# Seven half-width products in seven blocks instead of three, k's exponential in SBUF, and a written-out order, in a linear-attention plus feed-forward kernel

## The chip, the cores and the metric

The kernel runs on one core of one Trainium2 chip. The metric is the device time of one execution in microseconds; the figure used is the median of the runs. Engines are named as in the profile: PE (TensorE matmul), PEld (TensorE weight load), DVE (VectorE), ACT (ScalarE), POOL (GpSimd) and SP (SyncE, which issues the DMAs).

## The reference

Two stages. The first is a recurrence over 768 time steps for 4 batches and 8 heads of 48 dimensions, with a decay `w` between 0.8 and 0.95; the second a feed-forward layer from 384 to 2048 and back with a leaky ReLU.

```python
state = zeros((B, H, D, D))                      # B, H, S, D = 4, 8, 768, 48
for t in range(S):
    cur = einsum('bhd,bhe->bhde', u * k[:, :, t], v[:, :, t])
    y[:, :, t] = einsum('bhd,bhde->bhe', r[:, :, t], state + cur)
    state = w[:, :, t, :, None] * state + einsum('bhd,bhe->bhde', k[:, :, t], v[:, :, t])
x = y.transpose(0, 2, 1, 3).reshape(3072, 384)
h = x @ w_in                                      # 384 -> 2048
out = maximum(0.01 * h, h) @ w_out                # 2048 -> 384
```

## The kernel before, in words

**Chunks.** The 3072 rows are 24 chunks of 128 time steps. The first four chunks are done as two pairs (`pair`), the other twenty alone (`single`). In a single chunk, ScalarE takes the logarithm of w (L855), PE sums it over time (`cum`, L861, and totals, L864) into a PSUM bank `cp`, VectorE adds the logarithm again into `ci` in SBUF (L873), and ScalarE makes three exponentials: of the totals (`a`, L882), of `cp` in place (L887), and of `-ci` into a second PSUM bank, `ek` (L891). VectorE multiplies r by `cp` and k by `ek` into the two halves of `rk` (both in the helper `mult`, L545). `rk` is transposed into `rkT`, either on PE (L556) with a copy, or, for the 13 chunks in `RK_DMA`, by a DMA transpose that SP issues (L908). PE makes the scores (L1002; for chunks in `MERGED` two chunks at once), VectorE masks them (two masks per chunk, L932), and PE makes the state's sums (L942) and the output from state and masked scores (L968, L973). GpSimd works beside this: the bonus of u from products with k and r in a tile `ru` (L575, L579), reduced by VectorE into `dg` (L583) and multiplied by v into `vs` (L587), the cast of v (`vb`, L595), and the decayed state `sb` (L919). VectorE adds `vs` to the output (L618); the result is transposed into `xT`, on PE (L604) or by DMA (L987, chunks in `Y_DMA`).

**Feed-forward blocks.** The chunks are put into 15 blocks of one or two chunks (`blocks`). For each, 16 slices of the hidden layer are made by PE (`up`, L1168, 128 columns for a single, 256 for a pair), ScalarE applies the leaky ReLU into `g` (L1183), and PE makes the output of each chunk by 16 matmuls of 384 columns (`down`, L1198), copied out by VectorE or ScalarE (L1209, L1211) and stored (L1215).

**Seven products.** The last three pair blocks (`SEVEN_LAST = 3`) take `seven` instead of `down`. The pair's output is a product of a 2 x 2 arrangement of blocks (two chunks, two halves of the hidden slices) with another (two halves of the hidden slices, two halves of the 384 columns). It is made from seven products of halves instead of eight, each of 8 matmuls of 192 columns (L1098), at the price of four sums of 1024 columns on VectorE for each block (L1079), of three copies (L1112, L1114) and five adds (L1119) of 192 columns, and, once in the kernel, of four differences of the halves of w_out (`mix`, L1048). The sums and differences lie in tiles of the pool `in`, which otherwise holds loads.

**Weights and lead.** w_in is loaded in six pieces and w_out in four, between the loads of the pairs, and cast by VectorE, ScalarE or GpSimd (L488 to L492). Until the first blocks can run, PE is given matmuls of zeros where the plan sees a hole (L1240).

**The order.** Every operation is a step of a class `Plan`, with a cost per engine, a priority, its inputs and the buffers that it reads and takes. `Plan.order` runs a list scheduler over these costs: at each free engine it takes the ready step of the best priority, changed by a table of 1090 offsets (`RANK`), and a table `FORCE` fixes the engine of some steps. The result is the program order of each engine; each engine runs its own list in order, and SP's list is the order of the DMAs. A step that waits therefore holds everything behind it on its engine.

Of the kernel before, what the change touches and what calls it, by code (L numbers as in the profile page):

```python
# [8 lines left out]
F32 = mybir.dt.float32  # L9
BF16 = mybir.dt.bfloat16  # L10
# [5 lines left out]
class Buf:  # L16


    def __init__(self, pool, kind=None, wide=1):
        self.wide = wide  # L20
        self.pool, self.kind, self.users, self.t, self.free_at = pool, kind or pool, [], None, 0.0


class Plan:


    ENGINES = ("PE", "DVE", "ACT", "POOL", "SP")
# [4 lines left out]
    def __init__(self, limits, slack_from, slack, late):  # L32
        self.steps, self.limits, self.late = [], limits, late
        self.slack_from, self.slack = slack_from, slack
# [8 lines left out]
    def order(self, pools):  # L43
        n = len(self.steps)
        users = [[] for _ in range(n)]
        left = [len(s[3]) for s in self.steps]
        for i, s in enumerate(self.steps):
            for j in s[3]:
                users[j].append(i)
        bufs = {}  # L50
        for i, s in enumerate(self.steps):
            for b in (*s[4], *s[5]):
                bufs[id(b)] = b
        remain = {k: len(b.users) for k, b in bufs.items()}
        free_tiles = {p: [(0.0, k) for k in range(len(t))] for p, t in pools.items()}
        in_use = {}
        ready_at = [0.0] * n
        self.start, self.done, self.eng = [None] * n, [0.0] * n, [None] * n
        free = dict(self.BEGIN)
        ready = {e: [] for e in self.ENGINES}  # L60
        events = []
        dma_free, flying = 0.0, []

        def offer(i, t):
            for e in self.steps[i][0]:
                heapq.heappush(events, (t, 0, e, i))

        for i in range(n):
            if not left[i]:
                offer(i, 0.0)  # L70
        for e in self.ENGINES:
            heapq.heappush(events, (free[e], 1, e, -1))
        count, out = 0, []
        while events:
            now, kind, e, i = heapq.heappop(events)
            same = {e}
            if kind == 0 and self.start[i] is None:
                heapq.heappush(ready[e], (self.steps[i][2], i))
            elif kind == 2:
                in_use[i] -= 1  # L80
# [231 lines left out]
def kernel(  # L312
# [13 lines left out]
    L = 128  # L326
# [948 lines left out]
```

## Time and profile before

| | |
|---|---|
| time, median of 3 runs | 179.23 us (179.16 to 179.73) |
| span of the profiled execution | 177.7 us |
| the profiled execution's own time | not listed by itself; the median lies 1.5 us above the span |
| PE busy | 170.7 us, 96% |
| PE weight loads busy | 133.9 us, 75% |
| VectorE busy | 133.9 us, 75% |
| ScalarE busy | 115.6 us, 65% |
| GpSimd busy | 105.3 us, 59% |
| granted TensorE clock | full throughout |
| DMA | 34.24 MB, mean 193 GB/s |

Matmuls are pipelined and their modelled ends overlap the next one's start, so a busy PE is not PE at its peak. In a line of the timeline the first number is the start, the second the time until the end of the last merged instruction, and brackets hold the idle time before it and what ended that. In a group, the number after the comma is the mean duration of one instruction in ns. A line of the chain that ended last has a start, a length and what ran. "DMA to landing" is the time from issue to arrival.

### The profile page before, as it was taken

The page shows a single profiled execution, that of the slowest core. Times are in us where ns is not written, and L with a number is a line of the kernel's source. Part 1 is how long each engine was busy: PE and PEld are TensorE (multiplying, and loading weights), DVE is VectorE, ACT ScalarE, POOL GpSimd, SP SyncE. Part 2 cuts the span into 40 slices and gives each one's busy share as a digit, 9 for nine tenths or more (in the row PEclk, how much of TensorE's full clock was granted, in tenths as well). Part 3 has the DMA queues.
Part 4 walks back from the last instruction along what each step waited for, and adds up shares of the span by engine and source line. Part 5 has one row for each costly group of instructions (what it writes and reads, how often), then busy time and mean ns, then how long its engine had stood idle before and what let it go on. Part 6 is the DMA issues. An engine that isn't in the chain of part 4 may idle for free.

```text
span 177.7 us, 5379 instructions
## 1 busy us (share of the span) xinstructions
PE 170.7 (96%) x2106; PEld 133.9 (75%) x2110; DVE 133.9 (75%) x268; ACT 115.6 (65%) x258; POOL 105.3 (59%) x139
## 2 busy tenths in 40 slices
PE   7899899999999999999999999999999999999993
PEld 2456678766879767797788776788777798899992
DVE  7599744568987949979968888699779688776463
ACT  5679877764856687487497891288873677662820
POOL 5998554255897749993905994659884099100000
PEclk9999999999999999999999999999999999999999
DMA  5999999999999999997999999997999996613004
GB/s 142 262 283 341 338 377 325 234 197 168 193 146 210 171 189 191 194 227 171 221 185 209 197 147 222 205 177 155 191 208 148 241 207 160 159 24 111 4 22 157
DMA packets 115884, 34.24 MB, mean 193 GB/s; under 512 B 108305, under 2 KB 115090, under 8 KB 115858
## 3 DMA queue, kind: packets, MB, share of 16 engines
q1 hardware_dynamic: 115856, 33.89, 94.3%
q8 instruction: 16, 0.26, 0.7%
q14 instruction: 10, 0.08, 0.2%
q10 hardware_dynamic: 2, 0.00, 0.0%
HBM read 25.17 MB, written 4.72 MB: 168 GB/s over the span
## 4 chain that ended last, share of the span: by engine, by line
PE 74%; DMA 8%; SPq 5%; ACT 4%; DVE 3%; issue 3%; POOL 1%; DVEq 0%; ACTq 0%; POOLq 0%
PE ps L1168 29%; PE ps L1198 23%; PE ps L1098 8%; DMA in<-in_moe_w_in_dram 5%; SPq L630 4%; DMA in<-in_w_dram 3%; PE ps L1002 3%; PE ps L973 2%; ACT g L1183 2%; PE ps L861 2%; PE ps L556 2%; PE ps L968 2%; PE ps L942 1%; PE ps L604 1%; DVE in L1048 1%
## 5 line engine op out<-in xcount | busy, mean ns | idle before, releaser
L1168 PE MATMUL ps<-xT,w_in_b 128*128 128x256 bf16 (+1 forms) x720 | 73.3, 251 | 0.1
L1183 ACT ACTIVATE g<-ps 128x512 bf16<-128x512 f32 x96 | 55.9, 594 | 22.4 <-PE ps L1168 19.5
L1168 PEld LDWEIGHTS <-w_in_b 128*128 128x128 bf16 x720 | 57.6, 98 | 8.4 <-issue 0.3
L1198 PE MATMUL ps<-w_out_b,g 128*128 128x384 bf16 x288 | 56.5, 326 | 0.0
L1198 PEld LDWEIGHTS <-g 128*128 128x128 bf16 x288 | 25.1, 97 | 12.0
L545 DVE TENSOR_TENSOR rk<-in,ps 128x384 bf16<-128x384 f32 x48 | 25.3, 550 | 8.0 <-ACT ps L887 3.0
L575 POOL TENSOR_TENSOR ru<-in,ub 128x384 f32<-128x384 f32 x24 | 25.4, 1061 | 6.2 <-DMA in<-in_k_dram 6.1
L932 DVE TENSOR_TENSOR m<-ps,maskb 128x512 bf16<-128x512 f32 x40 | 25.3, 682 | 4.2 <-PE ps L1002 3.3
L595 POOL CAST vb<-in 128x384 bf16<-128x384 f32 x24 | 13.2, 553 | 22.3 <-DMA in<-in_v_dram 19.1
L579 POOL TENSOR_TENSOR ru<-ru,in 128x384 f32<-128x384 f32 x24 | 24.4, 1028 | 2.9 <-DMA in<-in_r_dram 2.4
L587 POOL TENSOR_TENSOR vs<-in,dg 128x384 f32<-128x384 f32 x20 | 17.0, 852 | 3.5 <-DVE dg L583 2.9
L919 POOL TENSOR_TENSOR sb<-s,a 128x384 bf16<-128x384 f32 x18 | 14.9, 830 | 3.3 <-ACT a L882 3.3
L873 DVE TENSOR_TENSOR ci<-ps,lw 128x384 f32<-128x384 f32 x20 | 11.1, 553 | 4.5 <-PE ps L861 1.8
L618 DVE TENSOR_TENSOR y<-ps,vs 128x384 bf16<-128x384 f32 x20 | 10.9, 553 | 4.5 <-PE ps L973 4.5
L583 DVE TENSOR_REDUCE dg<-ru 128x8 f32<-128x384 f32 x24 | 13.1, 544 | 0.7 <-POOL ru L579 0.6
L882 ACT ACTIVATE a<-ps 64x4 f32<-64x4 f32 x36 | 6.1, 168 | 11.6 <-DVE ci L873 8.9
L855 ACT ACTIVATE lw<-in 128x384 bf16<-128x384 f32 x20 | 10.1, 520 | 3.8 <-DMA in<-in_w_dram 3.6
L891 ACT ACTIVATE ps<-ci 128x384 f32<-128x384 f32 x20 | 9.7, 485 | 1.8 <-DVE ci L873 1.8
L887 ACT ACTIVATE ps<-ps 128x384 f32<-128x384 f32 x20 | 9.3, 467 | 0.5 <-DVE ci L873 0.3
L1240 PE MATMUL ps<-zeros 128*128 128x128 bf16 (+1 forms) x31 | 7.6, 351 | 1.6 <-DVE zeros L409 1.3
L556 PE MATMUL ps<-ident,rk 128*128 128x128 bf16 x88 | 8.4, 220 | 0.5 <-DVE rk L545 0.4
L1098 PEld LDWEIGHTS <-g 128*128 128x128 bf16 x96 | 8.1, 98 | 0.2
(105 smaller groups left out, 222.5 us busy)
## 6 DMA issues: line engine op xcount, KB each, us to landing
out_dram<-o SPq DMA_DIRECT2D x23, 192.0 KB, 2.7
in<-in_w_dram SPq DMA_DIRECT2D x20, 192.0 KB, 4.6
in<-in_v_dram SPq DMA_DIRECT2D x20, 192.0 KB, 4.9
in<-in_r_dram SPq DMA_DIRECT2D x20, 192.0 KB, 4.4
in<-in_k_dram SPq DMA_DIRECT2D x20, 192.0 KB, 4.6
in<-in_moe_w_out_dram SPq DMA_DIRECT2D x4, 768.0 KB, 8.7
in<-in_moe_w_in_dram SPq DMA_DIRECT2D x4, 384.0 KB, 7.8
in<-in_moe_w_in_dram SPq DMA_DIRECT2D x2, 768.0 KB, 8.5
```

The source lines that it names most:

```text
L545: (nc.gpsimd if e == "POOL" else nc.vector).tensor_tensor(out=o, in0=x, in1=i, op=ALU.mult)
L575: lambda e: nc.gpsimd.tensor_tensor(out=ru.t[:], in0=kv(), in1=ubv, op=ALU.mult),
L579: lambda e: nc.gpsimd.tensor_tensor(out=ru.t[:], in0=ru.t[:], in1=rv(), op=ALU.mult),
L583: lambda e: nc.vector.tensor_reduce(out=dg.t[:], in_=ru.t[:], axis=AX.X, op=ALU.add),
L587: lambda e: nc.gpsimd.tensor_tensor(out=vs.t[:], in0=vv(), in1=dg.t[:].unsqueeze(2).to_broadcast([128, H, D]), op=ALU.mult),
L595: {"POOL": 0.56}, lambda e: nc.gpsimd.tensor_copy(out=vb.t[:], in_=vv()),
L919: lambda e: nc.gpsimd.tensor_tensor(out=sb.t[:].rearrange("p g a d -> p (g a) d"), in0=s_in.t[:].rearrange("p g a d -> p (g a) d"), in1=a_ ...
L932: lambda e, par=par: nc.vector.tensor_tensor(out=m.t[:, par, :, :], in0=sc[par].t[:].rearrange("p (g t) -> p g t", g=NP), in1=maskb[:].uns ...
L1098: nc.tensor.matmul(o(), lhsT=x()[:, i, :], rhs=y()[:, i, :], start=fresh, stop=(stop and i == ii[-1]), skip_group_check=True)
L1168: nc.tensor.matmul(hp.t[:, a * N : (a + 1) * N], lhsT=w_in_b[:, t, (j + a) * 128 : (j + a + 1) * 128], rhs=xT[:, t, c0 : c0 + N], start=(a ...
L1183: lambda e, hp=hp, g=g, j=j, J=J, N=N: nc.scalar.activation(out=g.t[:, j : j + J, 0:N], in_=hp.t[:, 0 : J * N].rearrange("p (a n) -> p a n ...
L1198: nc.tensor.matmul(op.t[:, 0:DM], lhsT=g.t[:, j, off : off + 128], rhs=w_out_b[:, j, :], start=(j == 0), stop=(j == NJ - 1))
```

## The change

- `SEVEN_LAST` goes from 3 to 7, and the two neighbouring single blocks become a pair, so the last seven of 14 blocks, all pairs, take `seven`.
- k's exponential is written back into `ci` in SBUF, and the bank `ek` is no longer taken. The product with k can then run on VectorE or on GpSimd. In the order that is written out, 12 of the 20 run on GpSimd.
- `Plan.order` no longer schedules. It walks a list `ORDER` of all 1124 steps and assigns buffers; `FORCE` is a new table. Its costs only set the matmuls of zeros and which buffer is taken.
- Buffers: `in` 10 to 11, `ci` 2 to 3, `g` 3 to 4; the pairs' transposed tiles are taken from `g`; `xT` is six tiles of one block each instead of one tile for all rows.

What follows in the program: PE has 480 up matmuls of 256 columns and 192 of 128 (before: 432 and 288), 160 down matmuls (288) and 392 half-width products (168). The four differences of w_out stand much earlier in VectorE's list. SP's list has the loads in another order: the second pair's w and r go ahead of v, and one of the two wide w_in pieces comes first of the weights, ahead of the narrow ones.

```diff
-        self.pool, self.kind, self.users, self.t, self.free_at = pool, kind or pool, [], None, 0.0
+        self.pool, self.kind, self.users, self.t, self.free_at, self.seen = pool, kind or pool, [], None, 0.0, {}
...
     def order(self, pools):
...
+        for i in ORDER:
+            engs, fn, deps, reads, takes, wire = self.steps[i][0], *self.steps[i][1:2], *self.steps[i][3:]
...
+            e = FORCE.get(i) or next(iter(engs))
+            now = max(at[e], ready[i])
...
-RANK = {0: -309.63, 1: -310.62, 2: -303.35, 3: -175.12, 4: -176.12, 5: -3.85, 6: -313.07, 7: -303.34, 8:
...
+ORDER = [0, 1, 4, 2, 3, 1122, 5, 6, 7, 11, 14, 20, 13, 21, 12, 18, 19, 8, 25, 22, 26, 27, 23, 24, 40, 36, 15,
...
-    SEVEN_LAST = 3
+    SEVEN_LAST = 7
...
-    blocks = [2, 1, 1, 1, 1, 2, 2, 2, 2, 2, 1, 1, 2, 2, 2]
+    blocks = [2, 1, 1, 1, 1, 2, 2, 2, 2, 2, 2, 2, 2, 2]
...
-    xT = pool.tile([128, KT, NCH * L], BF16, name="xT")
-
-    make("in", 10, [128, 1536], F32)
+
+    make("in", 11, [128, 1536], F32)
...
-    make("ci", 2, [128, H, D], F32)
+    make("ci", 3, [128, H, D], F32)
...
-    make("rkT2", 2, [128, 2 * NP, 256], BF16)
...
-    make("g", 3, [128, NJ, max(blocks) * L], BF16)
+    make("g", 4, [128, NJ, max(blocks) * L], BF16)
+    make("xT", 6, [128, KT, max(blocks) * L], BF16)
...
-            rkT = Buf("rkT2")
+            rkT = Buf("g", "rkT2")
...
-            ci, ek = Buf("ci"), Buf("ps", "ek")
+            ci = Buf("ci")
...
             s_ek = step(
                 {"ACT": 0.53},
-                lambda e: nc.scalar.activation(out=heads(ek.t), in_=ci.t[:], func=AF.Exp, scale=-1.0),
-                P0, deps=[s_ci], reads=[ci], takes=[ek])
+                lambda e: nc.scalar.activation(out=ci.t[:], in_=ci.t[:], func=AF.Exp, scale=-1.0),
+                P0, deps=[s_ci], reads=[ci])
...
             s_k = step(
-                {"DVE": 0.55}, lambda e: mult(rk.t[:, 1, :, 0:D], heads(ek.t), kv()),
-                P0, deps=[kl, s_ek], reads=[slot, ek], takes=[rk])
+                {"DVE": 0.55, "POOL": 1.0}, lambda e: mult(rk.t[:, 1, :, 0:D], ci.t[:], kv(), e),
+                P0, deps=[kl, s_ek], reads=[slot, ci], takes=[rk])
```

More of the change, by code (lines that the diff above doesn't have):

```diff
@@ L1 @@
-import heapq
 from contextlib import ExitStack
@@ L49, in order @@
                 users[j].append(i)
-        bufs = {}
-        for i, s in enumerate(self.steps):
+        remain, free = {}, {p: [(0.0, k) for k in range(len(t))] for p, t in pools.items()}
+        for s in self.steps:
             for b in (*s[4], *s[5]):
[L53 to L58, printed above, removed]
```

225 lines of the change are left out of this document (87 added, 138 removed), and 190 rows, old and new, of tables (ORDER, RANK).

## The prediction

> **What bounds the kernel now.** I read the page's busy times first, then PE's waits, the windows, and the chain that ended last.
>
> ```profile
> PE 170.7 (96%) x2106; PEld 133.9 (75%) x2110; DVE 133.9 (75%) x268; ACT 115.6 (65%) x258; POOL 105.3 (59%) x139
> core 0: us, PE busy (x) PEld busy (x) DVE busy (x) ACT busy (x) POOL busy (x), PEclk, DMA share, GB/s
> 0.00:22.20 22.20, 18.69 (x256) 11.60 (x261) 17.73 (x47) 16.23 (x33) 17.51 (x35) 1.00 1.06 273
> 22.20:80.00 57.80, 57.49 (x727) 44.77 (x727) 42.20 (x81) 39.67 (x89) 40.34 (x50) 1.00 1.12 217
> 80.00:140.00 60.00, 59.81 (x714) 45.93 (x713) 49.69 (x90) 39.05 (x93) 38.26 (x44) 1.00 1.05 190
> 118.00:128.00 10.00, 10.00 (x113) 8.03 (x111) 9.59 (x13) 8.27 (x21) 9.33 (x9) 1.00 0.84 179
> 140.00:174.80 34.80, 34.72 (x416) 31.55 (x413) 24.01 (x53) 20.67 (x45) 9.21 (x11) 1.00 0.48 110
> 174.80:177.70 2.90, 0.00 (x0) 0.00 (x0) 0.31 (x1) 0.00 (x0) 0.00 (x0) 1.00 0.40 140
> ```
>
> From 22.2 us to the last matmul near 174.8 PE is idle for 0.31 + 0.19 + 0.08 = 0.58 us of 152.6, at the full granted clock. Busy matmuls overlap, so I also look at who ended PE's waits and how fast runs of equal matmuls go:
>
> ```profile
> PE ps L727 <- POOL vb L595: 0.7, 2, 0.4
> PE ps L942 <- ACT g L1183: 0.3, 1, 0.3
> PE ps L861 <- ACT lw L855: 0.2, 1, 0.2
> 26.05 1.34 PE ps L1168 x24
> 36.13 1.30 PE ps L1198 x8
> 75.33 1.31 PE ps L1168 x12
> 134.61 0.55 PE ps L1002 x16
> 138.44 0.20 PE ps L973 x8
> 168.78 5.95 PE ps L1098 x72
> ```
>
> The last six are pieces of the chain, each an unbroken run on PE. One matmul costs 1.34/24 = 0.056 us at 128 columns (up, single chunk), 1.31/12 = 0.109 at 256 (up, pair), 1.30/8 = 0.1625 at 384 (down), 5.95/72 = 0.0826 at 192 (a product of halves). So time goes by columns, and the kernel is bound by PE's stream: a lead of 22 us, 152.6 us without a gap, and 2.9 us for the last store. Whatever shortens the stream shortens the kernel, as long as the other engines keep up.
>
> **The sum's base.** The span is 177.7 us; the median of the three runs is 179.23, so I put 1.5 us around the span. The profiled execution has no time of its own on record.
>
> **PE's stream.** Four more pair blocks go by seven products: 4 x 32 = 128 down matmuls leave, 4 x 56 = 224 half-width ones come: -128 x 0.1625 + 224 x 0.0826 = -20.8 + 18.5 = -2.3 us. Two single blocks become one pair: 96 up matmuls of 128 columns become 48 of 256: -5.4 + 5.25 = -0.1. Nothing else on PE changes in number, but for filler (one matmul of zeros fewer), which runs only where PE would wait. **-2.4 us**, all of it on the path.
>
> A rule speaks against this term. The Trainium skill, "TensorE: Matmul & The Clock Gate", section "Back-to-back issue gap", gives a sustained 81 ns per matmul at 128 columns and 131 ns at 512, since weight loads share the budget; between these (an estimate from that page) 192 columns would cost 89 ns and 384 only 114, and the four blocks would lose 224 x 0.089 - 128 x 0.114 = 5.3 us. The trace's 56 ns at 128 columns and 162.5 at 384 contradict it.
>
> **The lead.** PE leaves it when the second pair's v has landed:
>
> ```profile
> 18.05 0.82 POOL L488 CAST w_in_b<-in 128x768 bf16<-128x768 f32 x1 [0.82 <-DMA in<-in_moe_w_in_dram]
> 20.68 0.96 POOL L595 CAST vb<-in 128x384 bf16<-128x384 f32 x2 [1.80 <-DMA in<-in_v_dram]
> 23.63 0.50 PE L812 MATMUL ps<-y,spread 64*128 64x384 bf16 x4
> in<-in_v_dram SPq DMA_DIRECT2D x2, 384.0 KB, 7.3
> ```
>
> Between the wide w_in piece (18.0) and v (20.68) two transfers of 384 KB land, 1.3 us each. In the changed order only one stands there (the same bytes precede the other pieces), so v should land 1.3 us sooner. Up to the bonus matmuls (L812) the changed stream holds six up matmuls and one of 384 columns fewer, 0.66 + 0.16 = 0.8 us, which are left for later: gain 1.3 - 0.8 = 0.5. Bounds: a gain of 1.3, if what is left over fills later holes of the lead, and a loss of 0.8, if the next cast of w_in (0.82), which now queues on GpSimd behind four steps on v, is what PE waits for next. The k, r and w loads of the first single chunk move between the weight pieces; PE needs them only after some 5 us more of up matmuls, which cover them. I take **-0.4**, near the shorter wait for v, which is what the row shows. Of the two later gaps (0.3 + 0.2 above), which other orders may close, I count **-0.2**.
>
> **VectorE and GpSimd.** Each added seven block brings four sums of 1024 columns, five adds and three copies of 192, for two copies of 384.
>
> ```profile
> L1079 DVE TENSOR_TENSOR in<-g 128x1024 bf16<-128x1024 bf16 x2 | 1.4, 686 | 0.7 <-ACT g L1183 0.7
> L1119 DVE TENSOR_TENSOR o<-ps,o 128x192 f32<-128x192 f32 x15 | 5.0, 352 | 1.8 <-PE ps L1098 1.3 <-ACT o L1114 0.3
> L545 DVE TENSOR_TENSOR rk<-in,ps 128x384 bf16<-128x384 f32 x48 | 25.3, 550 | 8.0 <-ACT ps L887 3.0 <-ACT ps L891 2.4 <-PE ps L668 1.1
> L932 DVE TENSOR_TENSOR m<-ps,maskb 128x512 bf16<-128x512 f32 x40 | 25.3, 682 | 4.2 <-PE ps L1002 3.3 <-ACT g L1183 0.8
> 156.10 1.28 DVE L932 TENSOR_TENSOR m<-ps,maskb 128x512 bf16<-128x512 f32 x2
> ```
>
> VectorE gains 16 x 0.69 + 20 x 0.35 = 18 us and gives 12 k products to GpSimd: -12 x 0.55 = -6.6. Net about +11 on 133.9, still 83% of a shorter span. GpSimd gets 12 products of about 1 us and one cast, ScalarE five short copies in all; on average neither nears PE. Back to back an instruction costs about 0.08 less (two masks in 1.28, not 1.36). Where VectorE is fullest decides. In the changed order that is near the end: between the last merged scores and the last-but-one chunk's output sum stand 19 VectorE instructions (8 masks, 4 sums, 5 of 384 columns including a reduction, 2 adds): 8 x 0.60 + 4 x 0.65 + 5 x 0.47 + 2 x 0.28 = 10.3 us, beside PE work of 12 up, 88 half, 17 score and 48 small matmuls: 1.3 + 7.3 + 0.6 + 1.4 = 10.6. It fits with 0.3 to spare, which one hand-over each way uses up. I expect PE to wait 0 to 0.5 there.
>
> The second price is what VectorE and GpSimd do to each other:
>
> ```profile
> 118.18 2.91 DVE L1048 TENSOR_TENSOR in<-w_out_b 128x1536 bf16<-128x1536 bf16 x2
> 120.35 1.60 POOL L579 TENSOR_TENSOR ru<-ru,in 128x384 f32<-128x384 f32 x1
> 126.18 0.83 POOL L919 TENSOR_TENSOR sb<-s,a 128x384 bf16<-128x384 f32 x1 [0.59 <-ACT a L882]
> 126.97 0.83 POOL L587 TENSOR_TENSOR vs<-in,dg 128x384 f32<-128x384 f32 x1
> 146.28 0.99 POOL L579 TENSOR_TENSOR ru<-ru,in 128x384 f32<-128x384 f32 x1
> 147.27 0.50 POOL L595 CAST vb<-in 128x384 bf16<-128x384 f32 x1
> 150.48 0.83 DVE L1079 TENSOR_TENSOR g<-g 128x1024 bf16<-128x1024 bf16 x1
> 150.71 0.96 POOL L595 CAST vb<-in 128x384 bf16<-128x384 f32 x1
> ```
>
> Beside VectorE instructions with both inputs in SBUF, GpSimd's product takes 1.60 instead of 0.99 and its cast 0.96 instead of 0.50: about 0.5 us lost per overlap; VectorE's sum takes 0.83 instead of 0.69. Until now such sums came when GpSimd was nearly done. The change puts 16 more, and the 8 k products that VectorE keeps (k's exponential is in SBUF now), into stretches where GpSimd works.
>
> Where that matters most: the k product of the last chunk is GpSimd's now. From the reduction that frees its ru tile to the end of that product GpSimd has ten steps in the changed order: ru and its product with r, two k products (four at 0.99, k's by the same kind's row), two sb and two vs (four at 0.83), two casts of v (0.50): 4.0 + 3.3 + 1.0 = 8.3 us, plus about three overlaps with sums, 1.5: 9.8. Behind the waiting k product on GpSimd stand the last chunk's ru, vs and v cast. Then SP transposes rk by DMA, and PE's last scores wait for that; two transposes of y follow later:
>
> ```profile
> DMA to landing us min/median/max: 3.0/3.9/5.7
> DMA to landing us min/median/max: 2.3/2.3/3.6
> 133.95 1.25 SPq L908 DMA_TRANSPOSE rkT<-rk  x1
> ```
>
> (The first row is rkT's, the second xT's.) 9.8 + 3.0, 3.9 or 5.7 make 12.8, 13.7 or 15.5 us. PE has 30 up, 104 half and 59 small matmuls beside it (scores at 0.034, the others at 0.025 to 0.16 by their columns): 3.3 + 8.6 + 2.0 = 13.9. Behind the waiting scores all of PE stands. Stall: 0 to 1.6; at the median none, but with only 0.2 to spare. For this and VectorE's stretch (0 to 0.5) together I take **+0.7**, a third of the upper ends, since in both the middle value just fits.
>
> The four differences of w_out (L1048) move from 118-124 us to where PE has done 48 to 60 us of its matmuls: some 6 us of VectorE in a stretch where it is less full (42.2 of 57.8); nothing on the path. Their two tiles of "in" and one per seven block are then withheld from loads, against one tile more; a late load would show as a wait of ScalarE for w. ek's PSUM bank goes free; the xT tiles become six that are reused, hidden as long as blocks finish in order (else a copy of 0.35 waits). The explicit order itself costs nothing on the chip.
>
> **Sum.** -2.4 - 0.4 - 0.2 + 0.7 = -2.3: span 175.4, time **176.9 us**.
>
> **Rivals.**
>
> 1. *VectorE becomes the bound (slower).* Place: the stretch between 80 and 143 us of PE's matmul work. There VectorE has, back to back, 48 instructions of 384 columns, 20 masks, 30 short adds and copies and 20 sums: 48 x 0.47 + 20 x 0.60 + 30 x 0.28 + 20 x 0.65 = 56 of 63 us. The sums and one k product, 21 instructions, have both inputs in SBUF. Price: what each loses to GpSimd, 0.14 us by the worst sum above, 0.99 if each waits for a whole GpSimd product. Spare are 7 us, and the gains are 3.0; the kernel ends slower than before from 10/21 = 0.48 us each. At 0.7 each: 179.2 - 3.0 + (14.7 - 7) = 183.9. The Trainium skill, "SBUF — State Buffer", in its section on the single rule of the shared pair, says for this that a tensor_tensor with two SBUF inputs and a GpSimd read exclude each other for the whole instruction; the trace agrees on GpSimd's side (0.61 and 0.46 us lost) and shows less on VectorE's (0.14). Against the rival: between 118 and 128 us VectorE was busy 9.59 of 10 with such instructions in it and GpSimd 9.33, and PE still 10.00. Chance 0.11.
> 2. *Late transfers eat the gain (no change).* The last rkT lands in 5.7 instead of 3.9: 1.6 late as above. Then the last xT: one add (0.55), the first transpose's issue (1.25) and a landing of 3.6 make 5.4 us, beside some 42 up matmuls, 4.6: 0.8 more. With 1.6 + 0.8 in place of 0.7 and without the 0.6 of the lead and the gaps: 179.2 - 2.4 + 2.4 = 179.2. A load held back by the withheld tiles does the same. For it: chunks wait for each other in a row. Against: medians fit. Chance 0.08.
>
> ```profile
> L1198 PEld LDWEIGHTS <-g 128*128 128x128 bf16 x288 | 25.1, 97 | 12.0
> ```
>
> 3. *Weight loads pace the half-width products*: at the 97 ns of a load, 224 x 0.097 - 20.8 = +0.9, so 179.2 + 0.9 - 0.1 = 180.0; this is how the rule on the issue gap above would act here. The run of 72 at 0.0826 speaks against it. Chance 0.01.
>
> That the change does not do what it says is excluded by the built order: 392 half-width products stand in it, 12 k products on GpSimd and 8 on VectorE.
>
> **How the numbers follow.** The forecast has 0.80. Its own range goes from all gains without a stall, 179.2 - 2.4 - 1.3 - 0.5 = 175.0, to both stalls' upper ends with no other gain, 179.2 - 2.4 + 0.5 + 1.6 = 178.9. Rival 2 lies at 179.2, so 175.0 to 179.4 takes in the forecast and rival 2 and leaves out rivals 1 and 3 (0.12) and what lies beyond the forecast's own bounds. What this kernel's measurement can tell from no change is 0.3%, 0.54 us: 178.7 to 179.8. Faster: the forecast less its upper end, 0.78. Same: that end, 0.02, and most of rival 2, 0.07. Slower: rivals 1 and 3 and the rest of 2, 0.13.
>
> **What would show it.** Right: in the profile after, windows in which PE is idle for about a microsecond in all between 22 us and a last matmul near 172.5; runs of half-width products at 0.083 us each; the second pair's v cast near 19.4 us instead of 20.68; the 1024-column sums at 0.7 to 0.85; VectorE some 11 us busier, GpSimd some 13. Wrong: the scores or the up matmuls of the last four chunks waiting over a microsecond for DMA, VectorE or GpSimd; sums of a microsecond and more; a first continuous run of PE that begins later than 22 us; ScalarE waiting for w in the middle of the span with PE idle behind it. The prediction falls if PE's idle time after the lead grows by more than the 2.4 us that its stream loses.

## The result, and the profile after

The changed kernel takes **182.14 us** (median of four runs, 181.18 to 182.62) against 179.37 for the kernel before (179.16 to 179.73, run beside it): a ratio of 1.0144, interval 1.0112 to 1.0177. It is **slower by 1.4%**; forecast was 176.9, faster. The profiled execution took 182.44 us, its span is 180.7 us, 3.0 us longer than before.

First the page's busy times and five windows of the changed kernel. The columns of a window are PE, PEld, DVE, ACT and POOL busy, then PE's clock.

```profile
PE 171.2 (95%) x2157; PEld 140.2 (78%) x2157; DVE 150.5 (83%) x293; ACT 113.8 (63%) x260; POOL 125.4 (69%) x152
0.00:22.20 22.20, 19.04 (x292) 12.12 (x294) 18.82 (x49) 14.63 (x30) 18.77 (x37) 1.00 1.07 266
22.20:47.00 24.80, 23.44 (x274) 17.81 (x271) 16.17 (x26) 16.06 (x34) 13.07 (x16) 1.00 1.02 253
47.00:96.00 49.00, 49.00 (x615) 38.39 (x614) 43.40 (x78) 35.95 (x87) 43.68 (x49) 1.00 1.13 192
96.00:158.70 62.70, 60.62 (x783) 54.09 (x781) 59.54 (x109) 36.99 (x92) 49.90 (x53) 1.00 0.94 174
158.70:177.90 19.20, 19.06 (x202) 17.82 (x200) 12.34 (x34) 10.18 (x19) 0.00 (x0) 1.00 0.22 70
```

VectorE is 16.6 us busier than before (forecast 11), GpSimd 20.1 (forecast 13). Before, PE's holes between 22 and 175 us came to 0.6 us; now there are 1.4 us before 47 us and 2.1 between 96 and 159, where VectorE is busy 95% of the time and GpSimd 80%. The ends of matmuls are modelled, so busy time hides a part of the waits. I therefore counted by starts too: from a time I take off the work that PE has begun by then, each matmul at the median distance between its start and the next one's for its shape, over the traces together, filler left out. What remains is the time that PE has lost so far:

```
us lost by PE at     30    50   100   130   150   170   begun in all
before             13.0  13.4  14.6  15.2  15.4  15.8   158.7
changed            12.7  14.7  15.8  18.6  20.0  21.3   156.2
```

Work: -2.5. Lead: -0.3. Between 30 and 170 us PE loses 8.6 us instead of 2.8: **+5.8**. Together +3.0, the difference of the spans. 1.6 of the 5.8 arise between 30 and 50 us, the rest after 100.

The chain that ended last says who holds PE there (share of the span by engine, the kernel before first, then the changed one and pieces of its chain: start, us, what):

```profile
PE 74%; DMA 8%; SPq 5%; ACT 4%; DVE 3%; issue 3%; POOL 1%; DVEq 0%; ACTq 0%; POOLq 0%
...
PE 42%; DVE 13%; SPq 13%; POOL 11%; DMA 10%; issue 7%; ACT 2%; DVEq 0%; POOLq 0%
...
98.09 1.47 DVE in L944
100.71 1.32 DVE in L944
111.28 1.27 DVE in L944
124.55 1.09 DVE in L944
126.96 1.31 DVE in L944
...
130.73 1.27 POOL sb L785
...
149.68 1.46 POOL rk L410
151.14 0.02 issue
151.16 4.71 DMA rkT<-rk
155.86 0.05 issue
155.91 0.40 PE ps L867 x8
...
158.69 9.83 PE ps L1033 x90
168.52 9.25 PE ps L963 x112
```

PE's share falls from 74% to 42%. From 98 to 130.7 us the chain lies mostly on VectorE, 20.5 of 32.6 us; its sums (L944) are 7.9 of these, the five shown at 1.1 to 1.5 us each. From 130.7 to 151.1 it lies on GpSimd; then on the DMA that transposes the last rk. Only from 158.7 on is it PE's again, with 9.25/112 = 0.083 us for a half-width product.

Why a sum takes 1.1 to 1.5 us is seen where the two engines' timelines are laid side by side (start, us, engine, line, operation; first VectorE, then GpSimd):

```profile
98.09 1.46 DVE L944 TENSOR_TENSOR in<-g 128x1024 bf16<-128x1024 bf16 x1 [0.62 <-ACT g L1048]
99.59 1.20 DVE L944 TENSOR_TENSOR g<-g 128x1024 bf16<-128x1024 bf16 x1
100.71 1.31 DVE L944 TENSOR_TENSOR in<-in,g 128x1024 bf16<-128x1024 bf16 x1
102.06 0.69 DVE L944 TENSOR_TENSOR in<-g,in 128x1024 bf16<-128x1024 bf16 x1
...
98.01 1.00 POOL L440 TENSOR_TENSOR ru<-in,ub 128x384 f32<-128x384 f32 x1
98.96 2.51 POOL L452 TENSOR_TENSOR vs<-in,dg 128x384 f32<-128x384 f32 x2
```

The first sum starts 0.08 us after GpSimd's ru and ends 0.54 us after it. Then GpSimd's two vs, 0.83 us each alone, take 2.51. The fourth sum has nothing beside it and takes 0.69. The two engines **take turns**. The groups of the sums, k products and ru products, by shape:

```profile
L944 DVE TENSOR_TENSOR in<-in,g 128x1024 bf16<-128x1024 bf16 x6 | 6.4, 1062 | 0.0
L944 DVE TENSOR_TENSOR in<-g 128x1024 bf16<-128x1024 bf16 x6 | 6.2, 1028 | 3.9 <-ACT g L1048 3.9
L944 DVE TENSOR_TENSOR g<-g 128x1024 bf16<-128x1024 bf16 x6 | 6.0, 1000 | 0.1
L944 DVE TENSOR_TENSOR in<-g,in 128x1024 bf16<-128x1024 bf16 x6 | 4.9, 814 | 0.1
L410 DVE TENSOR_TENSOR rk<-in,ci 128x384 bf16<-128x384 f32 x8 | 7.7, 966 | 0.0
L410 DVE TENSOR_TENSOR rk<-in,ps 128x384 bf16<-128x384 f32 x28 | 14.7, 547 | 1.7 <-ACT ps L753 1.1 <-ACT ps L554 0.6
L440 POOL TENSOR_TENSOR ru<-in,ub 128x384 f32<-128x384 f32 x24 | 26.0, 1089 | 7.3 <-DMA in<-in_k_dram 7.1
```

Mean of the 24 sums: 0.976 us. The six that ran with no GpSimd instruction beside them took 0.69, the other eighteen 1.07. A k product takes 0.966 us with its exponential in SBUF; r's product of the same shape, with one operand in PSUM, 0.547 as before. So VectorE loses 24 x 0.29 + 8 x 0.42 = 10.2 us in sums and k products. GpSimd loses 12 us in the same way, by its groups' means against what each takes alone.

### The profile page after: what moved, and what is told of

It is laid out like the page before. It is cut to its first block, busy times and chain, and to the rows that moved or that the text cites. A ratio compares the mean times of both kernels' runs of the same rounds, so it can differ in the third digit from the quotient of the medians.

```text
span 180.7 us, 5516 instructions
## 1 busy us (share of the span) xinstructions
PE 171.2 (95%) x2157; PEld 140.2 (78%) x2157; DVE 150.5 (83%) x293; ACT 113.8 (63%) x260; POOL 125.4 (69%) x152
## 4 chain that ended last, share of the span: by engine, by line
PE 42%; DVE 13%; SPq 13%; POOL 11%; DMA 10%; issue 7%; ACT 2%; DVEq 0%; POOLq 0%
PE ps L1033 17%; PE ps L1063 10%; PE ps L963 6%; SPq L711 5%; SPq L497 5%; DMA in<-in_moe_w_in_dram 4%; DVE in L944 4%; DMA in<-in_k_dram 3%; SPq L321 3%; DMA rkT<-rk 3%; POOL ru L440 2%; POOL rk L410 2%; POOL ru L444 2%; PE ps L867 2%; POOL sb L785 2%
## 5 line engine op out<-in xcount | busy, mean ns | idle before, releaser
L1033 PE MATMUL ps<-xT,w_in_b 128*128 128x256 bf16 (+1 forms) x672 | 70.5, 257 | 0.8 <-DVE xT L476 0.5
L1063 PE MATMUL ps<-w_out_b,g 128*128 128x384 bf16 x160 | 30.9, 326 | 0.8 <-DVE w_out_b L345 0.8
L452 POOL TENSOR_TENSOR vs<-in,dg 128x384 f32<-128x384 f32 x20 | 19.2, 962 | 6.1 <-DVE dg L448 3.8
L785 POOL TENSOR_TENSOR sb<-s,a 128x384 bf16<-128x384 f32 x18 | 17.3, 964 | 4.4 <-ACT a L748 2.6
L410 POOL TENSOR_TENSOR rk<-in,ci 128x384 bf16<-128x384 f32 x12 | 13.5, 1125 | 5.3 <-ACT ci L757 3.5
L410 DVE TENSOR_TENSOR rk<-in,ps 128x384 bf16<-128x384 f32 x28 | 14.7, 547 | 1.7 <-ACT ps L753 1.1
L963 PEld LDWEIGHTS <-in 128*128 128x128 bf16 x168 | 13.7, 98 | 0.9 <-DVE in L944 0.3
L757 ACT ACTIVATE ci<-ci 128x384 f32<-128x384 f32 x20 | 10.4, 520 | 5.2 <-DVE ci L739 5.1
L984 DVE TENSOR_TENSOR o<-ps,o 128x192 f32<-128x192 f32 x35 | 11.4, 350 | 1.5 <-ACT o L979 0.6
L979 ACT COPY o<-ps 128x192 f32<-128x192 f32 x14 | 4.5, 319 | 13.0 <-PE ps L963 8.8
```

The costliest lines, as they stand in the source:

```text
L410: (nc.gpsimd if e == "POOL" else nc.vector).tensor_tensor(out=o, in0=x, in1=i, op=ALU.mult)
L452: lambda e: nc.gpsimd.tensor_tensor(out=vs.t[:], in0=vv(), in1=dg.t[:].unsqueeze(2).to_broadcast([128, H, D]), op=ALU.mult),
L785: lambda e: nc.gpsimd.tensor_tensor(out=sb.t[:].rearrange("p g a d -> p (g a) d"), in0=s_in.t[:].rearrange("p g a d -> p (g a) d"), in1=a_ ...
L963: nc.tensor.matmul(o(), lhsT=x()[:, i, :], rhs=y()[:, i, :], start=fresh, stop=(stop and i == ii[-1]), skip_group_check=True)
L1033: nc.tensor.matmul(hp.t[:, a * N : (a + 1) * N], lhsT=w_in_b[:, t, (j + a) * 128 : (j + a + 1) * 128], rhs=xb.t[:, t, 0:N], start=(a == 0 ...
L1063: nc.tensor.matmul(op.t[:, 0:DM], lhsT=g.t[:, j, off : off + 128], rhs=w_out_b[:, j, :], start=(j == 0), stop=(j == NJ - 1))
```

## The experiments

Theory: the turns put 22 us more on two engines that are busy for 95% (VectorE) and 80% (GpSimd) of the time between 96 and 159 us, and PE waits for them. Rivals: GpSimd's queue with the k products in it is too long by itself; late loads or the written-out order cost the time. "Lost" below is PE's loss between 30 and 170 us, counted as above (before 2.8, changed 8.6). The ratio in each place is to the kernel before, run beside it.

**1. Sums of 128 columns.** Each sum does the first of its four or eight slices, and the products that would read the rest read that one (those of s3, which is written over g, still read all of g).

```diff
-    out=o()[:, i0:i1], in0=in0()[:, i0:i1], in1=in1()[:, i0:i1], op=op)
+    out=o()[:, i0:i0 + 1], in0=in0()[:, i0:i0 + 1], in1=in1()[:, i0:i0 + 1], op=op)
...
-    o(), lhsT=x()[:, i, :], rhs=y()[:, i, :], start=fresh, stop=(stop and i == ii[-1]),
+    o(), lhsT=x()[:, i if len(terms) > 1 or at in (2.5, 6.5, 10.5) else 0, :], rhs=y()[:, i, :], start=fresh, stop=(stop and i == ii[-1]),
```

> The changed kernel, but each of the sums of activations does only 128 of its 512 or 1024 columns, and the products read those 128 for all eight blocks; the rest of the sums is left out. Everything else, PE's stream included, stays. Theory (VectorE's two-input sums and GpSimd hold each other up, and the sums are the larger part): VectorE loses about 20 us of its 150.5, the excess of PE's stream over its own pace after 30 us falls from 8.6 us to 4 or less, and the time is 177 to 178.5 us against 182.1; GpSimd's products get shorter too (k product 1.13 toward 1.0). Rival A (GpSimd's queue at the end, with k products in it, is long by itself): the last rkT is still late, 180.5 to 182. Rival B (late loads, or the order itself): no change, 181.5 to 182.6.

Measured 177.97 us, ratio 0.991 (0.988 to 0.994), 4.2 us below the changed kernel; lost 4.2. The time is as the theory had it, against both rivals: GpSimd has all its work, and the order is the same. But VectorE is busy 139.1 us, 11.4 less and not the 20 expected. Its 32 sums take 15.0 us instead of 26.8; at the shortest time of each shape (0.22 narrow; 0.69 and 0.42 whole) they would take 7.0 and 19.9. So they lose 8.0 us to the turns against 6.9 in the changed kernel: what went is VectorE's own work, with 7.1 us of GpSimd's busy time. This run shows that the sums on VectorE hold PE; it can't tell the turns from a VectorE that is simply too full. The next two go further. The rows of two of the sums by tile (min/median/max in ns):

```profile
L944 DVE TENSOR_TENSOR in<-g x8: 216/486/1065, 96.6 to 163.0; 128x128 bf16<-128x128 bf16 x8
L944 DVE TENSOR_TENSOR g<-g x8: 218/398/1041, 97.4 to 163.3; 128x128 bf16<-128x128 bf16 x8
```

An eighth of the columns, 0.22 us alone, and still up to 1.07 us: the wait is one for GpSimd's instruction and does not shrink with the sum.

**2. Narrow products on GpSimd, and 3. the same with a fill.** In the single chunks GpSimd's two ru products do one head of eight (`W = 1`); in the second version the other seven heads are filled with a constant.

```diff
-    nc.gpsimd.tensor_tensor(out=ru.t[:], in0=kv(), in1=ubv, op=ALU.mult)
+    nc.gpsimd.tensor_tensor(out=ru.t[:, 0:W], in0=kv()[:, 0:W], in1=ubv[:, 0:W], op=ALU.mult)
+    nc.gpsimd.memset(ru.t[:, W:H], 0.5)      # third experiment only
```

> The changed kernel, but GpSimd's two products for ru do one head of eight in the single chunks; the other seven are left out. GpSimd loses about 35 to 40 us of its 125.4; VectorE's instructions are untouched. Theory: VectorE's sums get shorter by themselves, from a mean near 0.98 to 0.8 or less, its busy time falls by 3 us or more though its work is the same, and the time is 177 to 179. Rival A (only GpSimd's queue): the sums stay at 0.95 or more, and the time still falls to 178 to 180, by the stall before the last scores. Rival B (loads, order): 181.5 to 182.6.

> As the version with narrow products for ru (one head of eight), but GpSimd fills the other seven heads with a constant, by an instruction that reads nothing; the product of these heads is left out. GpSimd is busy longer than with the narrow products alone. Theory in its sharp form (what holds VectorE's two-input instructions is a GpSimd instruction that reads SBUF): the sums stay at the 0.88 us of the narrow version or below, none is lengthened beside a fill, time 179 to 180.5. Rival (any busy GpSimd instruction holds them): the sums go back to 0.95 or more, time 181 to 182.

Measured 179.87 (1.004, 1.001 to 1.007) and 179.85 (1.002, 0.999 to 1.005); lost 5.9 and 5.5. With the narrow products the 1024-column sums fall to means of 0.86 to 0.90, the k products on VectorE from 0.97 to 0.67, though VectorE's work is the same: its busy time goes from 150.5 to 143.5. The turns alone thus cost VectorE 7.0 us and more. The sums are 0.06 to 0.1 above what I expected, and the time lies 0.9 above the theory's 177 to 179, inside the range of rival A, whose sums of 0.95 or more did not show. The fill tells more. GpSimd is 12 us busier with it (107.1 against 94.8), and the time stays. Its rows, from the third version (first the product of one head, then the fill):

```profile
L441 POOL TENSOR_TENSOR ru<-in,ub x24: 278/288/1010, 6.5 to 147.3; 128x48 f32<-128x48 f32 x20, 128x384 f32<-128x384 f32 x4
L441 POOL MEMSET ru<- x20: 372/377/382, 30.0 to 148.0; 128x336 f32 x20
```

No fill was lengthened, by as little as 10 ns, though eight of the forty ran beside VectorE's two-input instructions, and a sum of 1024 columns that had a whole fill inside it took 0.69 us. (The 1010 ns in the first row is one of the four products of 384 columns; the longest of 48 took 995.) The turns are taken with GpSimd's instructions that read SBUF. That any busy GpSimd instruction holds VectorE is out; that GpSimd's shorter queue is a part of the 2.3 us gained is not, since it is still 18 us less busy than in the changed kernel. The Trainium skill, "SBUF — State Buffer", section "Who interferes with whom", says this: a VectorE instruction with two SBUF inputs contends with a GpSimd instruction that reads SBUF, not with one that only writes it, and calls the sharing an exclusive lock. The rows agree.

**4. All k products on VectorE**, in the changed order (`FORCE` of the twelve steps set to "DVE").

> The changed kernel in the same order, but the 12 k products of GpSimd are VectorE's too. Theory (VectorE is as full as it can be from 96 us on): VectorE gains 12 x 0.55 to 0.97 = 7 to 12 us, its waits move PE, and the time rises to 183 to 186, although GpSimd's chain before the last scores gets 4 us shorter. Rival A (GpSimd's queue with the k products in it is what ends last): 179.5 to 181. Rival B (loads, order): 181.5 to 182.6.

Measured 193.56 (1.078, 1.072 to 1.085); lost 20.6. Worse than any theory had it. VectorE is 7.1 us busier, but the loss is 12 us more: the places in the list suit a product in GpSimd's queue. In VectorE's it waits five times for ScalarE's exponential (3.5 us) with everything else behind it, and PE waits 3.6 us for rk. It speaks against rival A and shows nothing of the turns.

**5. and 6. The four added blocks by down matmuls.** 32 matmuls of 384 columns each, no sums, in the changed order: in the first version all at the first two of the six steps, in the second spread over all six.

```diff
+    if plain4:
+        t, j0, j1 = share[at]      # first version: 16 matmuls each at the first two steps
+        for j in range(j0, j1):
+            nc.tensor.matmul((b2 if t else b1).t[:, 0:DM], lhsT=g.t[:, j, t * L : (t + 1) * L],
+                             rhs=w_out_b[:, j, :], start=(j == 0), stop=(j == NJ - 1))
+        return
```

> The changed kernel in the same order, but the four added blocks of seven products are done as before, by 32 down matmuls of 384 columns each, at the places of the first two steps of products; their sums, short copies and adds are gone, two copies of 384 per block come instead. PE's work rises by 224 x 0.0826 and 128 x 0.1625: 2.3 us more. VectorE loses about 20 us. Theory (the sums cost more than the stream gains): excess after 30 us falls from 8.6 to 5 or less, time 180 to 182, no slower than the changed kernel. Rival A (k product on GpSimd and its queue): 184 to 185. Rival B (loads, order): 184.4, the changed kernel plus 2.3.

> The four added blocks by down matmuls of 384 columns again, in the changed order, but now the 32 matmuls of a block are spread over the places where its 56 half-width ones stood (8 for 16, 4 for 8, and 8 at the last place), so that PE's work lies where the order has it. No sums, short copies or adds in these blocks; three copies of 384 each. PE's work rises by 2.3 us. Theory (the sums, with what VectorE and GpSimd do to each other, cost more than the stream gains): 179.5 to 181.5, faster than the changed kernel's 182.1 although PE has more to do, and PE's stretch from 30 to 170 us has an excess of 4 to 5 us instead of 8.6. Rival A (GpSimd's k products and the queue before the last scores): 183.5 to 185. Rival B (the order's places): 184 to 187 as in the version before.

Measured 187.22 (1.042, 1.037 to 1.048) and 181.97 (1.014, 1.010 to 1.018). The first is above every range, and shows how much the list depends on where PE's work stands: with it gone from four of six places, PE loses 4.4 us between 150 and 160 us, behind masks, sums and an r product of VectorE (150.4 to 155.4 us) that the products used to cover. The second is the clean one: PE has 2.4 us more work and loses 5.4 instead of 8.6; the time is 0.2 us below the changed kernel's, within the spread of its runs. So the four blocks' sums, with their adds and short copies, cost 3.2 us of waits, and their stream gains 2.4: no gain. It came out above my 179.5 to 181.5, since more of the loss than I thought lies elsewhere.

**7. The kernel before with k's exponential in SBUF**, nothing else, and its order kept.

```diff
-    nc.scalar.activation(out=heads(ek.t), in_=ci.t[:], func=AF.Exp, scale=-1.0)
+    nc.scalar.activation(out=ci.t[:], in_=ci.t[:], func=AF.Exp, scale=-1.0)
...
-    mult(rk.t[:, 1, :, 0:D], heads(ek.t), kv())
+    mult(rk.t[:, 1, :, 0:D], ci.t[:], kv())
```

> The kernel before in its own order, with one part of the change alone: k's exponential is written over ci in SBUF, and the 20 k products, all on VectorE, read it there (their PSUM bank stays reserved). Theory: a product takes 0.55 us where GpSimd rests and 0.9 to 1.1 beside it, VectorE's busy time rises by 5 to 8 us from 133.9, and since VectorE has room in most of the span the time rises by little: 179.7 to 181. Rival (k's part costs nothing by itself): products at 0.55 to 0.6, 179.2 to 179.5.

Measured 181.41 (1.011, 1.007 to 1.014); lost 4.7, that is 1.9 more than before. This part alone makes the kernel slower by 1.8 us, more than I expected. Its group, and a stretch of VectorE through which the chain passes, as it does in the kernel before; the last line is the same k product there, with its exponential in PSUM:

```profile
L545 DVE TENSOR_TENSOR rk<-in,ci 128x384 bf16<-128x384 f32 x20 | 16.4, 821 | 3.5 <-ACT ci L891 2.6 <-DMA in<-in_k_dram 0.5 <-ACT lw L855 0.4
119.78 1.75 DVE L1048 TENSOR_TENSOR in<-w_out_b 128x1536 bf16<-128x1536 bf16 x1
121.46 0.55 DVE L873 TENSOR_TENSOR ci<-ps,lw 128x384 f32<-128x384 f32 x1
121.93 1.28 DVE L1048 TENSOR_TENSOR in<-w_out_b,in 128x1536 bf16<-128x1536 bf16 x1
123.13 0.54 DVE L545 TENSOR_TENSOR rk<-in,ps 128x384 bf16<-128x384 f32 x1
123.60 1.58 DVE L1048 TENSOR_TENSOR in<-w_out_b,in 128x1536 bf16<-128x1536 bf16 x1
125.10 1.34 DVE L545 TENSOR_TENSOR rk<-in,ci 128x384 bf16<-128x384 f32 x1
...
124.66 0.54 DVE L545 TENSOR_TENSOR rk<-in,ps 128x384 bf16<-128x384 f32 x1
```

The instructions around it take the same time in both kernels; the k product alone goes from 0.54 to 1.34 us. The 1.9 us for k's part and the 3.2 for the four blocks' sums would make 5.1 of the 5.8 us, but they come from two kernels with different orders and 20 against 8 k products on VectorE; that they add up is not shown.

**8. and 9. Eight exponentials back in PSUM**, for the chunks whose k product VectorE makes: first into r's bank, after r's product; then into a bank of its own, without that wait (the diff shows the second).

```diff
-    nc.scalar.activation(out=ci.t[:], in_=ci.t[:], func=AF.Exp, scale=-1.0), P0, deps=[s_ci], reads=[ci])
+    nc.scalar.activation(out=heads(ek.t) if n in KP else ci.t[:], in_=ci.t[:], func=AF.Exp, scale=-1.0),
+    P0, deps=[s_ci], reads=[ci], takes=[ek] if n in KP else [])
```

> The changed kernel, but for the eight chunks whose k product VectorE makes the exponential of k goes to PSUM, into the bank that r's exponential leaves after its product; ScalarE's step waits for that product. GpSimd's twelve stay. Theory: the eight products go from 0.97 to 0.55 us, VectorE loses 3.3 us, GpSimd about 1 to 2, and the time falls by 0.5 to 1.5 us from 182.1: 180.6 to 181.6. Rival (these products are no part of the cause, or the new wait of ScalarE takes it back): 181.8 to 183.

> The changed kernel in its order; for the eight chunks whose k product VectorE makes, ScalarE writes the exponential of k into a PSUM bank of its own, as before the change, with no wait for r's product. GpSimd's twelve stay. Theory: the eight products take 0.55 instead of 0.97 us, VectorE and GpSimd lose some 3 us less to each other, but most of these products stand before 85 us, where VectorE has room: 180.8 to 182. Rival (the products in SBUF are the main cause): 179.5 to 180.5.

Measured 187.73 (1.046, 1.042 to 1.049) and 182.9 (1.017, 1.012 to 1.022); lost 14.6 and 10.1. Both are misses. The first pays for the new wait: PE waits 3.7 us for rk between 55 and 85 us. The second has no such wait, but the bank it takes turns the order of banks, and PE loses 3.7 us between 50 and 80 us behind a late load of r and the differences of w_out. In a list made for other banks, taking the turns away from eight products isn't enough; what they cost there stays unmeasured.

**10. The two w_out casts at 43.6 us on ScalarE** (`FORCE` of two steps), since PE waited 0.8 us for them on VectorE.

> The changed kernel in its order, but the two casts of w_out at 43.6 us, which took VectorE 1.18 us each beside GpSimd (0.56 alone) and for which PE waited 0.8 us, are ScalarE's. Theory: about 1 us of the 1.7 us that PE loses between 40 and 45 us goes, the rest of the span is unchanged: 181.0 to 181.7. Rival (the late load of k, not the casts, holds PE there): 181.8 to 182.6.

Measured 181.79 (1.012, 1.010 to 1.014), lost 7.8. Inconclusive: PE now waits 1.2 us for ScalarE's casts, and has lost as much at 50 us as before the edit.

**11. New orders of the changed work.** Same steps, tiles and bank counts; the list, and the engine of some 40 steps that may go to more than one, are new after 26 or 34 us. They come from a search that moves steps about and keeps what shortens a plan made from the durations in the traces, with one rule added: VectorE's two-input instructions and casts from SBUF, and GpSimd's reading ones, take turns. All but the first also have later transfers in the plan; the last has eight of the exponentials in a bank of their own besides.

```diff
-ORDER = [0, 1, 4, 2, 3, 1122, ...
+ORDER = [0, 1, 4, 2, 3, 1122, ...      # the same up to the lead's end, then new
-FORCE = {4: "DVE", 6: "DVE", ...
+FORCE = {4: "DVE", 6: "DVE", ...
```

> The changed kernel with the same steps, tiles and banks; only the order of the steps after the lead, and the engine of some 37 steps that may go to more than one, are new (17 of the 20 k products on GpSimd instead of 12). The order was chosen with one rule added to what it is counted by: an instruction of VectorE that takes two inputs from SBUF (sums, k products, differences) or casts from there, and an instruction of GpSimd that reads SBUF, take turns. Theory (the loss is those turns falling on the path, because the order was made as if both engines ran freely): the turns are still taken, but PE does not wait for them; its excess after 30 us falls from 8.6 to 3.5 to 5 us, the time is 176 to 178.5, faster than both kernels. Rival A (VectorE is simply full with seven blocks of sums): 180 to 182. Rival B (any other order is as good or worse): 181 to 184.

> The changed kernel's steps, tiles and banks; the order after 34 us and the engine of 40 steps are new, chosen with the rule that VectorE's instructions with two SBUF inputs and GpSimd's reading ones take turns, and now also with every transfer landing 2 us later than planned, as the loads of the first reordered version did. Eight of the 20 k products are GpSimd's. Theory (the loss is an order that counted neither the turns nor late loads; the work itself fits): the excess of PE's stream after 30 us falls from 8.6 to 4 or 5 us, the time is 177 to 178.8, faster than before. Rival A (seven blocks of sums are too much for VectorE, whatever the order): 180.5 to 182. Rival B (the transfers, at over 0.9 of their engines' time up to 130 us, bound every order): 180 to 181.5, with DMA ahead of VectorE in the chain.

> As the run before, another such order, begun from the first reordered version (twelve k products on GpSimd; order new from 26 us on). Theory: 177 to 179. Rivals as before: 180 to 182.

> The changed kernel's steps in a further order, begun from the second reordered version (179.8) and chosen with transfers 2.6 us late, order new from 34 us on. Theory (turns and late loads are the loss, and an order that allows for both gets the stream's 2.4 us): 177.5 to 179. Rival A (VectorE too full in any order): 179.5 to 181.

> The changed kernel with the exponential of k in a PSUM bank of its own for the eight chunks whose product VectorE made, in an order chosen by the same two rules from 34 us on. Theory: eight turns fewer to take than in the reordered changed kernel, 177.5 to 179.5. Rival (the bank that it takes is missed elsewhere, or VectorE too full in any order): 180 to 182.

Measured, in this order: 181.21 (1.010, 1.007 to 1.013), **179.78** (1.001, 0.998 to 1.003), 182.04 (1.014, 1.010 to 1.017), **179.86** (1.001, 0.999 to 1.003) and 182.13 (1.014, 1.010 to 1.018). The first gained 0.9 us, and its chain after 130 us is of late loads: k landed 4.64 us after its issue, v 4.82, the last rkT 4.76. With late loads in the plan, two of the three lists of exactly the changed work got it done 2.3 us sooner than the changed kernel's own list, as fast as before; PE's loss is 6.0 and 5.3. The third gained nothing; it loses 3.2 us between 50 and 100 us, 1.4 of them in one wait for a late rkT. The last list of all, with fewer turns to take, gained nothing either. So a better order is worth up to 2.3 us, and the theory is half right: no list was faster than before. VectorE's busy time between 96 and 158 us, the third figure after the stretch's length, explains a part of that; in order the kernel before, the changed one, the list at 179.78, that at 179.86:

```profile
96.00:158.00 62.00, 61.81 (x739) 49.05 (x738) 50.57 (x91) 40.43 (x96) 39.24 (x44) 1.00 0.98 180
```

```profile
96.00:158.00 62.00, 59.92 (x768) 53.42 (x766) 59.43 (x109) 36.65 (x91) 49.90 (x53) 1.00 0.94 172
```

```profile
96.00:158.00 62.00, 60.48 (x791) 54.43 (x789) 61.38 (x118) 36.66 (x95) 47.25 (x50) 1.00 0.89 177
```

```profile
96.00:158.00 62.00, 61.37 (x796) 55.31 (x795) 59.03 (x116) 36.16 (x92) 51.23 (x53) 1.00 0.95 181
```

In the list at 179.78 VectorE has 0.6 us to spare in 62, and PE loses 3.0 us between 100 and 150: there rival A of these runs, VectorE too full in any order, fits. The list at 179.86 leaves VectorE 3.0 us to spare and loses 1.4 in that stretch; 2.4 of its 5.3 us are lost between 30 and 50 us, where VectorE is far from full and the chain runs over a load of w_out that landed 9.37 us after its issue. So VectorE's load alone does not explain both, and that no order does better than the kernel before is not shown.

**12. Control: new orders of the kernel before**, by the same search.

> A control: the kernel before with the same steps, its order after the lead chosen in the same way with the same rule, written out as a list. It has three blocks of sums and no k product with two SBUF inputs, so few turns to take. Theory: little to gain, 178.3 to 179.4 against 179.4. Rival (a new order helps any version as much): 177 or less.

> The control again: the kernel before, its order after 34 us chosen by the same two rules and written out. Theory (few turns to take, so little to gain): 178.5 to 180. Rival (the way of ordering, not the turns, is what helps): 177 or less. Against both: 181 or more, if its own planner's order fits late transfers better than the list.

> The control once more. The two reordered versions of the kernel before had lost its list of forced engines on the way to an explicit order, so that some 20 steps ran on another engine than in that kernel, and its filler in the lead had changed; neither could tell anything of the order. This one has the engines and the filler of the kernel before up to 34 us, and after that an order and eight changed engines, by the same two rules (turns, transfers 2 us late) as the reordered changed kernel. Theory (the kernel before has few turns to take): 178.5 to 180. Rival (the way of ordering helps any version by as much as it helped the changed kernel, 2.4 us): 176.5 to 177.5.

The first two, 185.85 and 184.4 us, tell nothing of the order: by the engines' counts at least 27 and 25 steps ran on another engine than in the kernel before (the expectation of the third says some 20), and the lead's filler had changed, so that PE had lost 2.4 and 3.5 us more by 30 us. The third has both as before: 179.16 (0.9972, 0.9945 to 0.9998), 0.35 us gained. The search helps the changed kernel by 2.3 us, the kernel before by 0.35, at the edge of what can be told. So the search does not help every version alike. That the changed list lacked above all the turns, of which the kernel before has few, fits this but is not shown: with the turns alone in the plan the list gained 0.9 us, the rest came with the later transfers, no list was made with these and without the turns, and the order of the kernel before may simply have been the better one to begin with. The third control is the fastest version of the whole work found here, and it has nothing of the change in it.

## Why the prediction was wrong, step by step

- **PE's stream, -2.4.** Right. The work begun is 2.5 us less, a half-width product takes 0.083 us (9.25/112), and the rule of the Trainium skill ("TensorE: Matmul & The Clock Gate", "Back-to-back issue gap") did not show.
- **The lead, -0.4.** Right. The second pair's v cast starts at 19.48 us (19.4 forecast; 20.68 before), and PE has lost 0.3 us less by 30 us.
- **The two later gaps, -0.2.** Half right, and small beside what follows. They stood at 66 and 128 us; between 47 and 96 us PE now has no idle time, between 96 and 159 it has 2.1 us. New, and in no term of the sum, are 2.0 us lost between 30 and 50 us (0.4 before). There a k product (1.36 us beside ru) and two w_out casts (1.18 us each, 0.56 alone) take turns with GpSimd, and a load of k lands late.
- **VectorE and GpSimd, +0.7: this is the step that failed.** Together with the gaps it stood at +0.5 and measured +5.8: 1.6 of these between 30 and 50 us, the rest after 100. The mechanism was in the text; the term that was mis-sized is "VectorE's sum takes 0.83 instead of 0.69". That is 0.14 us lost per sum, from one sum; three in that trace had GpSimd beside them, and this was the longest. Eighteen sums beside GpSimd lost 0.38 on the mean, up to 0.77. And the k products that VectorE keeps were put at the 0.55 us of a product with a PSUM operand; they take 0.97. A better row stood in the prediction already: two differences of w_out in 2.91 us, 1.46 each for 1536 columns, where the sum's own rate gives 0.69 x 1.5 = 1.03. That is 0.4 lost per instruction, the right price. VectorE's stretch near the end, put at 0 to 0.5 us of waits, lost PE 4.2 us together with GpSimd's queue between 100 and 150 us (0.8 before). How the 5.8 us divide between VectorE's own added work, the turns, late transfers and the places in the list stays open; experiments 2, 3 and 7 show the turns in it, 1 and 6 the sums, and 11 that up to 2.3 us hang on the list.
- **GpSimd's ten steps before the last scores, 9.8 us, then 3.9 for the DMA.** The size was right: ru at 141.28 to the k product's end at 151.13 is 9.85 us, and rkT landed 4.7 us later. But GpSimd came to these steps late: the chain passes to it from VectorE at 130.7, after 1.76 us in which it was idle, and up to 141.28 it does ten instructions, two of them lengthened (an sb of 1.28 us and a k product of 1.44), with one wait of 1.05 us for ScalarE.
- **The differences of w_out, "nothing on the path".** Right: they stand between 62.6 and 75.5 us, and PE was busy 49.00 of 49.00 us between 47 and 96, though two took 1.75 us each. In the kernel before and in experiments 7 and 9, with other places or waits, the chain does pass through them.
- **Rival 1, VectorE becomes the bound, chance 0.11.** This is in the main what happened, in the place that it named; 1.6 of the 5.8 us were lost elsewhere. Its price was near (the rows: 0.38 per sum beside GpSimd). Its threshold, 0.48 us per instruction, was too high: it let VectorE's loss use up all of VectorE's idle time before PE would wait, and left out what GpSimd loses in the same turns. I set its chance by "PE still 10.00" between 118 and 128 us of the kernel before, a stretch with four such instructions; the change has 24 sums of 1024 columns and 8 k products. And the chain of the kernel before speaks for the rival there: from 119.6 to 128.4 us it lies on VectorE and ScalarE, with 2.3 us of two differences of w_out in it, and it ends in PE's wait of 0.2 us for the logarithm of w. In experiment 7 a k product 0.8 us longer in just that stretch comes on top.
- **The sign.** The condition in the last line of the prediction held: PE's idle time after the lead grew by 3.0 us (0.6 to 3.6), more than the 2.4 us that its stream loses.

## What to carry to other kernels

Before an instruction on VectorE gets a second operand in SBUF, count the GpSimd instructions beside it that read SBUF, and charge each meeting with the rest of the other engine's instruction (0.4 us a sum here), whatever the size of the new one. An order written out by hand or found by search is only as good as the plan that it was found with: the same work took 182.1 us in the changed kernel's list, 181.2 in one planned with the turns counted, and 179.8 in the two best of three planned with turns and later transfers. And a saving on the engine that bounds a kernel is worth nothing if it is paid on one that is 83% busy, and 95% in the stretch where it is paid.

## What the runs showed of the hardware that I had not expected

- A VectorE sum of 128 columns, 0.22 us alone, took up to 1.07 us beside GpSimd: the wait is set by the other engine's instruction.
- A GpSimd fill of 336 columns (372 to 382 ns) was never lengthened, while a product of 48 columns beside it, 0.29 us alone, went up to 1.0 us.
- VectorE's reduction of ru, which reads one SBUF operand, stayed at 0.54 us beside GpSimd in every run; its casts from SBUF did not (0.56 alone, 1.18).
